# Gated linear attention ahead of a two-level expert layer: attention rebuilt chunk by chunk over all head pairs

## The chip, the cores and the metric

One core of one Trainium2 chip runs the program. The metric is the device time of one execution in microseconds (us); the time given for a kernel is the median of several runs, and the profile comes from one execution of its own.

## The reference

The first half is a gated linear attention over 4 batches, 8 heads, 768 positions and 48 values per head. The second is an expert layer over the 3072 tokens of width 384: a token picks one of 4 groups, then one of 4 experts in it, and goes through that expert's two matrices.

```python
for t in range(S):                       # attention, per batch and head
    state = alpha[t][:, None] * state + outer(k[t], v[t])
    y[t] = q[t] @ state
x = y as (B*S, H*D)
g_idx = argmax(x @ w_group); g_w = softmax value of it
e_idx = argmax(x @ w_expert[g_idx]); e_w = softmax value of it
out = g_w * e_w * (relu(x @ w1[g, e]) @ w2[g, e])
```

Everything is float32.

## The kernel before

**Attention.** The work is done in chunks of 128 positions, 6 to a batch, so that the recurrence becomes matrix products. Two heads share the partitions: one in 0 to 47, the other in 64 to 111 (`heads`, 112 partitions with the gap). The main loop (lines 339 to 362) runs over 16 combinations `j` of a batch and a pair of heads and does all six chunks of a pair before the next pair begins.

- `decayed(j)` (143) makes running products of the decays over 64-step segments with 12 scans (L150), their reciprocal over all 768 positions (L152), and from these the scaled queries and keys on VectorE and GpSimd: `qp` and `kp`, relative to a segment's start, `qs` and `ks`, relative to a chunk's, and `ka` for the second half of a chunk against the first (L155 to L175).
- `scores` (208) takes two chunks at a time: per head and chunk a 128x128 product (L214) and a 64x64 one over its upper right part (L216), both contracting over the 48 partitions of one head; VectorE applies the causal mask on the way out of the accumulator (L220).
- `states` (178) transposes the keys (L188), copies them to memory (L190), multiplies them with the values (L194), and runs the recurrence over the chunks in 48x48 pieces (L201, L203).
- `outputs` (226) adds the state's part (L232) and the scores' part (L237, 48 columns of values streamed against 128x128 masked scores) and copies the rows out (L241).
- `gates(b)` (244) comes once a batch, after its last pair: it transposes the rows (L250), takes the logits (L258), makes the choice of group and expert in some thirty small VectorE instructions (L269 to L323), counts each token's rank by two products (L310, L311), and scatters the rows, six tiles of 128, to the experts' slots in memory (L326).

A float32 product shows as two MATMUL rows with a weight load (LDWEIGHTS) each, a transpose as one.

**Experts.** Loop over 16 experts of 224 slots (425): `columns` transposes the fetched rows (L377), `hidden` does the first matrix (L390), `result` the second (L399), and a scatter writes the output (L404). Rows are fetched three experts ahead (L413).

**Order.** A scheduler fixes each engine's order ahead of time; within an engine instructions run in that order. The SyncE queue carries `load` (L141), the blanking of the slots (L348) and the weights (L120, L122); three experts' weights have buffers.

Of the kernel before, what the change touches and what calls it, by code (L numbers as in the profile page):

```python
# [20 lines left out]
SEG = 64  # L21
# [3 lines left out]
def gla_then_hierarchical_moe(  # L25
# [4 lines left out]
    wr_d: bass.AP,  # L30
    w1_d: bass.AP,
# [11 lines left out]

    nc = tc.nc
    B, H, D, _, S = qka_d.shape
    HP = H // 2
    D2 = 2 * D
    R = 64 + D
    NC = S // P
    NSEG = S // SEG  # L50
# [15 lines left out]
    wp = ctx.enter_context(tc.tile_pool(name="weights", bufs=3))  # L66
# [8 lines left out]
    slots_d = dp.tile([NE * N, XW], F32, name="slots_d")  # L75

# [13 lines left out]
    zeros = cp.tile([P, SEG], F32, name="zeros")  # L90
# [15 lines left out]
    wr = cp.tile([P, DC, NL], F32, name="wr")  # L106
# [20 lines left out]
    with ExitStack() as gla:  # L127
        NB = 2
        buf = gla.enter_context(tc.tile_pool(name="buf", bufs=1))
        prep = gla.enter_context(tc.tile_pool(name="prep", bufs=2))  # L130
        work = gla.enter_context(tc.tile_pool(name="work", bufs=3))
        qka = [buf.tile([P, 3, S], F32, name=f"qka{i}") for i in range(NB)]
        state = [buf.tile([P, NC - 1, D2], F32, name=f"state{i}") for i in range(NB)]
        for i in range(NB):
            nc.gpsimd.memset(qka[i], 1.0)
            nc.gpsimd.memset(state[i], 0.0)

        def load(j):
            b, hp = divmod(j, HP)
            for t in range(2):  # L140
                nc.sync.dma_start(out=qka[j % NB][heads[t]], in_=qka_d[b, 2 * hp + t])  # L141

        def decayed(j):
            t = qka[j % NB]
            q, k, a = (t[0:R, n, :] for n in range(3))
            cum = prep.tile([P, S], F32, name="cum")[0:R]
            inv = prep.tile([P, S], F32, name="inv", bufs=1)[0:R]
            for s in range(NSEG):
                sl = slice(s * SEG, (s + 1) * SEG)
                nc.vector.tensor_tensor_scan(out=cum[:, sl], data0=a[:, sl], data1=zeros[0:R],  # L150
                                             initial=1.0, op0=ALU.mult, op1=ALU.add)
            nc.vector.reciprocal(out=inv, in_=cum)  # L152
# [8 lines left out]
            def halves(z):  # L161
                z = z.rearrange("p (c h s) -> p c h s", h=2, s=SEG)
                return z[:, :, 0, :], z[:, :, 1, :]
# [175 lines left out]
        for j in range(PAIRS):  # L339
            b, hp = divmod(j, HP)  # L340
            if j + 1 < PAIRS:
                load(j + 1)
# [201 lines left out]
```

## Time and profile before

| | |
|---|---|
| median of 3 runs | 883.52 us (882.74 to 884.09) |
| profiled execution, its own time | 883.95 us |
| its span in the trace | 882.3 us |
| busy: PE, weight loads, VectorE (DVE), ScalarE (ACT), GpSimd (POOL) | 86%, 68%, 34%, 9%, 14% |
| moved by DMA | 90.29 MB |

Times inside the trace count from the start of the span. A busy PE is a modelled figure: a matmul row lasts from its issue to its modelled end and overlaps the next, so the pace of a row of matmuls is read from the distance of their starts.

### The profile page before, as it was taken

To read this page: it belongs to the slowest core of one execution; us is meant where nothing else is said; L and a number is where in the kernel's file an instruction comes from. 1 tells how busy PE (TensorE), PEld (TensorE's weight loads), DVE (VectorE), ACT (ScalarE), POOL (GpSimd) and SP (SyncE) were. 2 spreads that over 40 slices of the span, in tenths; PEclk is the share of its full clock that TensorE was granted. 3 is DMA by queue.
4 is the path that set the end of the run, shared out by engine and by line. 5 is a ranking of instruction groups with operands and counts; after the bars stand their busy time and mean duration, and the time that the engine had idled before them with its cause. 6 is when DMAs were issued, how large, how long until landed. Compare 5 with 4: busy or idle time off the path is not lost. (4 is left out here: it accounts for less than half of the span.)

```text
span 882.3 us, 8155 instructions
## 1 busy us (share of the span) xinstructions
PE 760.9 (86%) x3152; PEld 601.2 (68%) x3152; DVE 301.5 (34%) x805; ACT 80.0 (9%) x197; POOL 121.5 (14%) x126
## 2 busy tenths in 40 slices
PE   0099998799996999995999951999999999999995
PEld 0067777577775777784778741777777777777773
DVE  0466665625358434629253251011111111111100
ACT  0000111010010011010100000011111000001110
POOL 3111111032011121102300002010000001001000
PEclk9999999999999999999999999999999999999998
DMA  9844623230223030222000003255545554455100
GB/s 347 236 114 110 183 41 94 41 68 28 41 41 94 10 76 10 41 40 59 37 0 1 0 10 103 85 193 212 202 177 180 206 202 172 179 179 195 59 15 15
DMA packets 16646, 90.29 MB, mean 102 GB/s; under 512 B 2821, under 2 KB 6410, under 8 KB 10464
## 3 DMA queue, kind: packets, MB, share of 16 engines
q1 hardware_dynamic: 8464, 70.03, 26.1%
q10 hardware_dynamic: 4816, 10.29, 3.3%
q0 software_dynamic: 3328, 9.47, 3.0%
q8 instruction: 25, 0.41, 0.2%
q14 instruction: 13, 0.11, 0.0%
HBM read 74.77 MB, written 15.78 MB: 103 GB/s over the span
## 5 line engine op out<-in xcount | busy, mean ns | idle before, releaser
L214 PE MATMUL bank<-qp,kp 48*128 48x128 f32 x384 | 147.1, 498 | 43.8 <-DVE tot L175 43.8
L399 PE MATMUL bank<-w,hT 128*96 128x384 f32 (+1 forms) x512 | 168.2, 487 | 0.0
L390 PEld LDWEIGHTS bank<-xt_e,w 128*128 128x128 f32 x768 | 147.2, 193 | 5.7 <-issue 2.4
L390 PE MATMUL bank<-xt_e,w 128*128 128x224 f32 x768 | 150.4, 356 | 0.5 <-DVE xt_e L379 0.5
L214 PEld LDWEIGHTS bank<-qp,kp 48*128 48x128 f32 x384 | 92.5, 308 | 68.3 <-issue 47.3
L399 PEld LDWEIGHTS bank<-w,hT 128*96 128x96 f32 (+1 forms) x512 | 89.2, 177 | 70.0 <-issue 38.3
L237 PE MATMUL bank<-v,sm 128*128 128x48 f32 x384 | 98.0, 401 | 0.0
L237 PEld LDWEIGHTS bank<-v,sm 128*128 128x128 f32 x384 | 93.0, 330 | 4.8 <-issue 1.6
L220 DVE TENSOR_TENSOR sm<-bank,causal 128x256 f32<-128x256 f32 x96 | 39.8, 422 | 142.4 <-PE bank L216 141.1
L216 PE MATMUL bank<-qp,ka 48*64 48x64 f32 x384 | 87.5, 337 | 0.1
L216 PEld LDWEIGHTS bank<-qp,ka 48*64 48x64 f32 x384 | 52.6, 200 | 39.8 <-issue 38.1
L152 DVE RECIPROCAL inv<-cum 112x768 f32<-112x768 f32 x16 | 79.2, 4952 | 0.4
L402 DVE TENSOR_SCALAR yo<-bank,xg 128x384 f32<-128x384 f32 (+1 forms) x32 | 19.7, 615 | 154.1 <-PE bank L399 154.1
L404 POOL DMA_INDIRECT out_dram<-yo,dst x32 | 30.4, 950 | 300.2 <-DVE yo L402 300.2
L392 ACT ACTIVATE hT<-bank 128x448 f32<-128x448 f32 x64 | 34.8, 543 | 306.4 <-PE bank L390 306.4
L155 POOL TENSOR_TENSOR qp<-qka,cum 112x768 f32<-112x768 f32 x16 | 28.9, 1804 | 201.1 <-PE bank L216 62.5
L232 PE MATMUL bank<-state,qs 112*128 112x96 f32 x160 | 53.9, 456 | 0.0
L150 DVE TENSOR_TENSOR_SCAN cum<-qka,zeros 112x64 f32<-112x64 f32 x192 | 41.9, 274 | 32.3 <-DMA qka<-in_qka_dram 32.3
L194 PE MATMUL bank<-v,kn 128*112 128x96 f32 x160 | 39.9, 416 | 9.0 <-ACT kn L190 9.0
L194 PEld LDWEIGHTS bank<-v,kn 128*112 128x112 f32 x160 | 32.2, 298 | 16.4 <-ACT kn L190 14.5
L232 PEld LDWEIGHTS bank<-state,qs 112*128 112x128 f32 x160 | 41.3, 327 | 3.0 <-issue 1.1
L241 ACT COPY x<-bank 128x192 f32<-128x192 f32 x48 | 15.3, 320 | 275.6 <-PE bank L237 275.6
(103 smaller groups left out, 402.1 us busy)
## 6 DMA issues: line engine op xcount, KB each, us to landing
w<-in_w_dram SPq DMA_DIRECT2D x32, 1536.0 KB, 6.7
qka<-in_qka_dram SPq DMA_DIRECT2D x32, 432.0 KB, 6.6
slots_d<-blank SPq DMA_DIRECT2D x1, 5404.0 KB, 27.3
v<-in_v_dram ACTq DMA_DIRECT2D x4, 1152.0 KB, 5.2
xg<-slots_d ACTq DMA_DIRECT2D x16, 193.0 KB, 6.5
xg<-slots_d ACTq DMA_DIRECT2D x16, 144.8 KB, 6.3
out_dram<-yo,dst POOLq DMA_INDIRECT x32, 2.6
slots_d<-x,place POOLq DMA_INDIRECT x24, 2.9
```

Of the source, the lines that this page charges most:

```text
L150: nc.vector.tensor_tensor_scan(out=cum[:, sl], data0=a[:, sl], data1=zeros[0:R], initial=1.0, op0=ALU.mult, op1=ALU.add)
L152: nc.vector.reciprocal(out=inv, in_=cum)
L194: nc.tensor.matmul(z[0:R, c * D2:(c + 1) * D2], lhsT=kn[:, i, :], rhs=v[:, c, hp * D2:(hp + 1) * D2], start=True, stop=True)
L214: nc.tensor.matmul(z[:, o:o + P], lhsT=kp[r, c:c + P], rhs=qp[r, c:c + P], start=True, stop=True)
L216: nc.tensor.matmul(z[0:SEG, o + SEG:o + P], lhsT=ka[r, c // 2:c // 2 + SEG], rhs=qp[r, c + SEG:c + P], start=True, stop=True)
L220: nc.vector.tensor_tensor(out=s, in0=z[:, 0:2 * P].rearrange("p (c i) -> p c i", c=2), in1=causal[:, None, :].to_broadcast([P, 2, P]), op= ...
L232: nc.tensor.matmul(z[:, i * D2:(i + 1) * D2], lhsT=qs[:, c * P:(c + 1) * P], rhs=st[0:R, c - 1, :], start=True, stop=False, skip_group_che ...
L237: nc.tensor.matmul(z[:, i * D2 + t * D:i * D2 + (t + 1) * D], lhsT=sm[t][:, i, :], rhs=v[:, c, h * D:(h + 1) * D], start=(c == 0 and t == ...
L390: nc.tensor.matmul(z[:, k * n:(k + 1) * n], lhsT=w1[:, dc, f * P:(f + 1) * P], rhs=xt[:, dc, 0:n], start=(dc == 0), stop=(dc == DC - 1))
L392: nc.scalar.activation(out=hT[:, f0:f0 + 2, 0:n], in_=z[:, 0:2 * n].rearrange("p (f t) -> p f t", f=2), func=AF.Relu)
L399: nc.tensor.matmul(zy[0:n, 0:DM], lhsT=hT[:, f, c0:c0 + n], rhs=w2[:, f, :], start=(f == 0), stop=(f == FC - 1))
L404: nc.gpsimd.indirect_dma_start(out=out, out_offset=bass.IndirectOffsetOnAxis(ap=dst, axis=0), in_=yo[0:n], in_offset=None, bounds_check=N ...
```

## The change

The attention is rewritten; the expert part keeps its instructions.

- **Input layout.** The host packs a unit of three chunks (half a batch) of a head pair into 112 partitions: queries, keys, decays with a zero at each chunk's first position, and those first decays apart. The loop runs over 24 chunks `n`; each does all four head pairs.
- **Decays.** `decayed(u, p)` uses two scans of 384 positions: one backwards, relative to the chunk's end (`rev`), one forwards that begins at its reciprocal (`cq`). The reciprocal is taken of three values. Keys times `rev` and queries times `cq` are two GpSimd products; ScalarE copies the queries of each head into a tile `qb` that is zero in the other head's partitions.
- **Scores.** One product per head pair and chunk: 112 partitions, both heads side by side in 256 columns. The 64x64 products go; a mask covers 512 columns.
- **State and outputs.** One state tile for all pairs; the update is two additions and two multiplications. The outputs come out transposed (48 rows of a head by 128 positions), with the values as weights.
- **Rows and logits** come from one product per pair with a matrix that holds a selector and the routing weights (`to_rows`); the transposes and copies of `gates` go.
- **Routing** of the last batch is cut into groups of 3, 2 and 1 tiles, `choose` and `send` are apart, and the scatters write to views that are declared disjoint.
- **Weights** have two buffers in place of three; those of expert e+2 are asked for between `hidden(e)` and `result(e)`.

```diff
-    wp = ctx.enter_context(tc.tile_pool(name="weights", bufs=3))
+    wp = ctx.enter_context(tc.tile_pool(name="weights", bufs=2))
...
+    slots_by_tile = dram_disjoint_views(slots_d, NT)
...
+        def decayed(u, p):
...
+            nc.vector.tensor_tensor_scan(out=flat(rev)[:, ::-1], data0=az[:, US:0:-1],
+                                         data1=flat(ends)[:, ::-1], initial=0.0,
+                                         op0=ALU.mult, op1=ALU.add)
+            nc.vector.reciprocal(out=st[:, :, 0], in_=rev[:, :, 0])
+            nc.vector.tensor_tensor_scan(out=flat(cq), data0=az[:, 0:US], data1=flat(st),
+                                         initial=0.0, op0=ALU.mult, op1=ALU.add)
+            nc.vector.tensor_tensor(out=tot[:, :, p], in0=rev[:, :, 0], in1=a0, op=ALU.mult)
+            nc.gpsimd.tensor_tensor(out=flat(kp[:, p]), in0=k, in1=flat(rev), op=ALU.mult)
+            nc.gpsimd.tensor_tensor(out=flat(qp[:, p]), in0=q, in1=flat(cq), op=ALU.mult)
+            for i, r in enumerate(heads):
+                nc.scalar.copy(out=qd[r, p, :, i, :], in_=qp[r, p])
...
+        def scores(n):
...
+                    nc.tensor.matmul(z[:, (p - g) * 2 * P:(p - g + 1) * 2 * P],
+                                     lhsT=kp[:, p, c, :],
+                                     rhs=qd[:, p, c].rearrange("r h s -> r (h s)"),
+                                     start=True, stop=True)
+                nc.vector.tensor_tensor(out=sm[:, 2 * g:2 * g + 4, :],
+                                        in0=z.rearrange("p (h i) -> p h i", h=4),
+                                        in1=causal[:, None, :].to_broadcast([P, 4, P]),
+                                        op=ALU.mult)
...
+        def next_state(n, st):
...
+            for p in range(HP):
+                nc.tensor.transpose(zt[:, p * R:(p + 1) * R], kp[:, p, c, :], ident[0:R, 0:R])
+            nc.scalar.copy(out=kt, in_=zt[:, 0:HP * R])
...
+                nc.tensor.matmul(z[0:R, p * D2:(p + 1) * D2], lhsT=kt[:, p * R:(p + 1) * R],
+                                 rhs=v[:, bc, p * D2:(p + 1) * D2], start=True, stop=True)
...
+                nc.vector.tensor_tensor(out=new[r, :, cols], in0=st[r, :, cols],
+                                        in1=add[r, :, i, :], op=ALU.add)
+                nc.vector.tensor_tensor(
+                    out=new[r, :, cols], in0=new[r, :, cols],
+                    in1=tot[r, n % UC, :, None].to_broadcast([D, HP, D]), op=ALU.mult)
...
+        def outputs(n, sm, st):
...
+                nc.tensor.matmul(z[0:R, p * P:(p + 1) * P], lhsT=st[:, p, :], rhs=qp[:, p, c, :],
+                                 start=(p == 0), stop=False, skip_group_check=True)
...
+                    nc.tensor.matmul(z[r, p * P:(p + 1) * P],
+                                     lhsT=vs[b][:, bc, h * D:(h + 1) * D], rhs=sm[:, h, :],
+                                     start=False, stop=True, skip_group_check=True)
...
+        def to_rows(n, yt):
...
+                nc.tensor.matmul(z[:, p * W:(p + 1) * W], lhsT=yt[:, p, :], rhs=wr[:, p, :],
+                                 start=True, stop=True)
...
+        cuts = [0, NC // 2, NC - 1, NC]
+        for c0, c1 in zip(cuts, cuts[1:]):
+            groups[(B - 1) * NC + c1 - 1] = (B - 1, c0, c1)
...
         hT = hidden(w1, xt, CAP)
+        if e + 2 < NE:
+            load_weights(e + 2, e + 2)
...
-        if e + 3 < NE:
-            load_weights(e + 3, e + 3)
```

TensorE (PE) in the attention, before: two chunks' scores of one pair end here and the next pair's begin. Numbers tell tiles apart.

```order
L232 MATMUL bank_249<-state0_118,qs_152 128x96
L237 MATMUL bank_249<-v_126,sm0_232 128x48
L237 MATMUL bank_249<-v_126,sm1_239 128x48
L214 MATMUL bank_289<-qp_275,kp_276 128x128
L214 MATMUL bank_296<-qp_275,kp_276 128x128
L216 MATMUL bank_289<-qp_275,ka_281 64x64
L214 MATMUL bank_289<-qp_275,kp_276 128x128
L216 MATMUL bank_289<-qp_275,ka_281 64x64
L216 MATMUL bank_296<-qp_275,ka_281 64x64
L214 MATMUL bank_296<-qp_275,kp_276 128x128
L216 MATMUL bank_296<-qp_275,ka_281 64x64
```

The same engine after the change, one chunk from its keys' transposes on (L218 transposes, L224 keys by values, L265 rows and logits, L200 scores, L244 and L249 outputs):

```order
L218 MATMUL bank_619<-ident_73,kp_397 128x112 x4
L224 MATMUL bank_626<-v_298,kt_620 112x96 x4
L265 MATMUL bank_635<-wr_100,yt_563 128x116 x4
L200 MATMUL bank_718<-qb0_124,kp_397 128x256 x2
L200 MATMUL bank_722<-qb0_124,kp_397 128x256 x2
L244 MATMUL bank_726<-qp_396,state2_128 112x128 x4
L249 MATMUL bank_726<-sm_595,v_298 48x128 x8
```

Four kinds of product of 48 to 128 columns that alternate have become runs of four or eight of one kind; the longest stretch without a wait for ScalarE is rows, scores and outputs.

VectorE (DVE) in the attention, before, from the scans of one pair to those products that end the next pair's preparation (scans print as SCALAR_TENSOR_TENSOR here):

```order
L150 SCALAR_TENSOR_TENSOR cum_390<-qka0_116,zeros_86 112x64 x10
L296 COPY x_774<-token_f_90 128x6
L152 RECIPROCAL inv_391<-cum_390 112x768
L201 COPY state1_119<-bank_303 48x48 x2
L203 SCALAR_TENSOR_TENSOR state1_119<-state1_119,tot_287,bank_303 48x48 x8
L220 TENSOR_TENSOR sm0_338<-bank_333,causal_78 128x256
L220 TENSOR_TENSOR sm1_345<-bank_340,causal_78 128x256
L220 TENSOR_TENSOR sm0_359<-bank_354,causal_78 128x256
L220 TENSOR_TENSOR sm1_366<-bank_361,causal_78 128x256
L156 TENSOR_TENSOR kp_406<-qka0_116,inv_391 112x768
L173 TENSOR_TENSOR qs_409<-qp_405,cum_390 112x6x64
L170 TENSOR_TENSOR ks_410<-kp_406,cum_390 112x6x64
```

VectorE after the change, around one mask (L204) and one state update (L230):

```order
L181 SCALAR_TENSOR_TENSOR rev_399<-qka_289,ends_119 112x384
L184 RECIPROCAL starts0_122<-rev_399 112x3
L187 TENSOR_TENSOR tot_398<-rev_399,qka_289 112x3
L185 SCALAR_TENSOR_TENSOR cq_400<-qka_289,starts0_122 112x384
L204 TENSOR_TENSOR sm_349<-bank_354,causal_78 128x512
L181 SCALAR_TENSOR_TENSOR rev_409<-qka_291,ends_119 112x384
L184 RECIPROCAL starts1_123<-rev_409 112x3
L187 TENSOR_TENSOR tot_398<-rev_409,qka_291 112x3
L185 SCALAR_TENSOR_TENSOR cq_410<-qka_291,starts1_123 112x384
L181 SCALAR_TENSOR_TENSOR rev_466<-qka_293,ends_119 112x384
L230 TENSOR_TENSOR state2_128<-state1_127,bank_380 48x4x48 x2
```

The large reciprocal is gone; masks and state updates stand between the scans of the next unit.

SyncE's queue at the program's start, before:

```order
L120 DMA w1_386<-in_w1_dram 128x3072
L348 DMA slots_d_72<-blank_103 112x16x772
L141 DMA qka0_116<-in_qka_dram 48x2304 x2
L141 DMA qka1_117<-in_qka_dram 48x2304 x2
L122 DMA w2_387<-in_w2_dram 128x3072
```

And after the change:

```order
L157 DMA qka_136<-in_qka_dram 112x1156
L157 DMA qka_138<-in_qka_dram 112x1156
L157 DMA qka_140<-in_qka_dram 112x1156
L157 DMA qka_142<-in_qka_dram 112x1156
L157 DMA qka_189<-in_qka_dram 112x1156
L397 DMA slots_d_72<-blank_103 112x16x772
```

The first unit's four inputs and one of the second now stand ahead of the 5404 KB of blanking; a matrix of weights and the blanking stood ahead of the first input before.

## Rows read from the trace of the kernel before

**Rows 1.** Stretches: length, busy (count) of PE, PEld, DVE, ACT, POOL; PEclk, DMA, GB/s.
```profile
0.00:43.80 43.80, 0.04 (x1) 0.07 (x1) 9.61 (x20) 1.79 (x2) 8.99 (x24) 1.00 0.88 293
43.80:515.70 471.90, 434.15 (x1762) 351.31 (x1763) 242.14 (x634) 42.99 (x129) 76.27 (x65) 1.00 0.22 53
515.70:548.20 32.50, 3.13 (x17) 2.84 (x15) 11.78 (x58) 0.45 (x2) 5.84 (x6) 1.00 0.15 49
548.20:882.30 334.10, 323.53 (x1376) 247.03 (x1376) 37.99 (x95) 34.78 (x64) 30.40 (x32) 0.99 0.42 153
```

**Rows 2.** Groups of PE at 548 us, then at 561 us: count, busy us, mean ns, idle.
```profile
L377 PE MATMUL bank<-ident,xg 128*128 128x128 f32 x3 | 0.9, 430 | 25.4 <-DMA xg<-slots_d 25.4
...
L377 PE MATMUL bank<-ident,xg 128*128 128x128 f32 x3 | 0.5, 273 | 0.0
```

**Rows 3.** Two stretches of 4.6 us in expert 0's L390, same columns.
```profile
550.10:554.70 4.60, 4.60 (x12) 4.20 (x13) 0.23 (x2) 0.00 (x0) 0.00 (x0) 1.00 0.35 97
555.10:559.70 4.60, 4.60 (x26) 4.60 (x25) 0.00 (x0) 1.04 (x3) 0.00 (x0) 1.00 0.00 0
```

**Rows 4.** Timeline of PE in the attention: start us, length us, what.
```profile
131.16 0.79 PE L214 MATMUL bank<-qp,kp 48*128 48x128 f32 x2
131.88 0.47 PE L216 MATMUL bank<-qp,ka 48*64 48x64 f32 x2
132.28 0.79 PE L214 MATMUL bank<-qp,kp 48*128 48x128 f32 x2
...
144.88 1.93 PE L250 MATMUL bank<-ident,x 128*128 128x128 f32 x8
...
152.78 4.03 PE L258 MATMUL bank<-wr,xt 128*128 128x20 f32 x18 [2.84 <-DVE xt L254]
...
167.27 0.63 PE L188 MATMUL bank<-ident,ks 112*128 112x112 f32 x2
168.39 1.06 PE L194 MATMUL bank<-v,kn 128*112 128x96 f32 x4 [0.49 <-ACT kn L190]
```

**Rows 5.** Groups of VectorE by line and shape, whole span.
```profile
L220 DVE TENSOR_TENSOR sm<-bank,causal 128x256 f32<-128x256 f32 x96 | 39.8, 422 | 142.4 <-PE bank L216 141.1
L203 DVE SCALAR_TENSOR_TENSOR state<-state,tot,bank 48x48 f32<-48x48 f32 x128 | 33.6, 263 | 4.1
L150 DVE TENSOR_TENSOR_SCAN cum<-qka,zeros 112x64 f32<-112x64 f32 x192 | 41.9, 274 | 32.3 <-DMA qka<-in_qka_dram 32.3
L449 DVE TENSOR_TENSOR_SCAN ends<-more,zeros 128x16 f32<-128x16 f32 x1 | 0.2, 182 | 0.0
L152 DVE RECIPROCAL inv<-cum 112x768 f32<-112x768 f32 x16 | 79.2, 4952 | 0.4
```

**Rows 6.** Single lines: shortest, median and longest ns of one.
```profile
L170 DVE TENSOR_TENSOR ks<-kp,cum x16: 547/550/1197, 43.8 to 479.1; 112x384 f32<-112x384 f32 x16
...
L175 DVE TENSOR_TENSOR tot<-cum x16: 160/164/799, 43.5 to 480.2; 112x6 f32<-112x6 f32 x16
```

**Rows 7.** A group of GpSimd, whole span.
```profile
L169 POOL TENSOR_TENSOR ka<-kp,cum 112x384 f32<-112x384 f32 x16 | 15.4, 960 | 156.0 <-DVE kp L156 151.6 <-DVE tot L175 4.4
```

**Rows 8.** Timeline of the start, all engines but PE.
```profile
4.95 19.33 SPq L141 DMA_DIRECT2D qka<-in_qka_dram  x4
...
35.07 2.29 DVE L150 TENSOR_TENSOR_SCAN cum<-qka,zeros 112x64 f32<-112x64 f32 x12 [32.27 <-DMA qka<-in_qka_dram]
```

**Rows 9.** Timeline of the last batch's routing.
```profile
518.52 0.28 DVE L261 COPY lg<-bank 128x120 f32<-128x120 f32 x1 [1.75 <-PE bank L258]
...
542.53 0.97 POOL L326 DMA_INDIRECT slots_d<-x,place  x1 [2.14 <-DMA slots_d<-x,place]
545.23 3.70 ACTq L413 DMA_DIRECT2D xg<-slots_d  x8
...
548.19 1.36 PE L377 MATMUL bank<-ident,xg 128*128 128x128 f32 x6 [25.35 <-DMA xg<-slots_d]
```

**Rows 10.** DMA issues: queue, count, size, median us to landing.
```profile
w<-in_w_dram SPq DMA_DIRECT2D x32, 1536.0 KB, 6.7
```

More of the change, by code (lines that the diff above doesn't have):

```diff
@@ L30, in gla_then_hierarchical_moe @@
     wr_d: bass.AP,
+    d_head: int,
     w1_d: bass.AP,
@@ L127, in gla_then_hierarchical_moe @@
     with ExitStack() as gla:
-        NB = 2
         buf = gla.enter_context(tc.tile_pool(name="buf", bufs=1))
+        inp = gla.enter_context(tc.tile_pool(name="inp", bufs=5))
         prep = gla.enter_context(tc.tile_pool(name="prep", bufs=2))
[L131 to L136, printed above, removed]
@@ new lines, in gla_then_hierarchical_moe @@
+        ends = buf.tile([R, UC, P], F32, name="ends")
+        nc.gpsimd.memset(ends, 0.0)
+        nc.gpsimd.memset(ends[:, :, P - 1:P], 1.0)
+        starts = [buf.tile([R, UC, P], F32, name=f"starts{i}") for i in range(2)]
+        qb = [buf.tile([R, HP, UC, 2, P], F32, name=f"qb{i}") for i in range(2)]
+        state = [buf.tile([R, HP, R], F32, name=f"state{i}") for i in range(3)]
+        for t in starts + state:
+            nc.vector.memset(t, 0.0)
+        nc.vector.memset(qb[0], 0.0)
@@ new lines, in scores @@
+        def scores(n):
+            u, c = divmod(n, UC)
+            _, kp, qd, _ = ready[u]
+            sm = work.tile([P, H, P], F32, name="sm")
+            for g in range(0, HP, 2):
+                z = bank()
+                for p in (g, g + 1):
+                    nc.tensor.matmul(z[:, (p - g) * 2 * P:(p - g + 1) * 2 * P],
[6 more added lines that the diff above has]
+                                        op=ALU.mult)
+            return sm
@@ L338, in gla_then_hierarchical_moe @@
-        load_v(0)
[L339 to L342, printed above, removed]
-            if hp == 0:
-                xs[b] = xp.tile([P, NC, XW], F32, name="x")
-                if b + 1 < B:
-                    load_v(b + 1)
-            if j == 1:
+                    out=slots_by_tile[b * NC + c0 + c],
+                    out_offset=bass.IndirectOffsetOnAxis(ap=place[:, c:c + 1], axis=0),
+                    in_=x[:, c0 + c, :], in_offset=None, bounds_check=NE * N - 1,
@@ new lines, in gla_then_hierarchical_moe @@
+        for p in range(HP):
+            load(0, p)
+        load_v(0)
+        for p in range(HP):
+            decayed(0, p)
+        for p in range(HP):
+            load(1, p)
+        LAST = B * NC
+        sm, st, yt = scores(0), state[0], None
+        for n in range(LAST):
+            u, c = divmod(n, UC)
+            if c == 0 and u + 1 < NU:
+                for p in range(0, HP // 2):
+                    decayed(u + 1, p)
+            elif c == 1 and u + 1 < NU:
+                for p in range(HP // 2, HP):
+                    decayed(u + 1, p)
+                if u + 2 < NU:
+                    for p in range(HP):
+                        load(u + 2, p)
+            if n == 1:
```

331 lines of the change are left out of this document (157 added, 174 removed).

## Prediction

> **What bounds the kernel now.** I read the busy time by stretch first [rows 1]. The reader is to see four stretches with different limits: 43.8 us before the first matmul, 471.9 us of attention in which PE is busy for 434, 32.5 us of routing in which PE does nothing, and 334.1 us of experts in which PE is busy for 323.5. The change rebuilds the first three. In the attention VectorE is busy for 242 us and waits for PE at every mask: L220 idles 142.4 us ahead of its 96 instructions [rows 5]. So PE sets the attention's length.
>
> The next question is at which clock PE did that. The clock column says 1.00 all along [rows 3], but the rows contradict it: the same transpose L377 takes 430 ns at 548 us and 273 ns at 561 us [rows 2], and L390 issues 12 matmuls in 4.6 us before 555 us and at least twice as many in the 4.6 us after [rows 3]. So for the time ahead of 555 us the column can't be taken at its word: there the engine was at the lower of its two levels (1.2 of 2.4 GHz). In the attention eight L250 transposes of that same 128x128 shape take 1.93 us, some 0.22 each and a drain [rows 4], the pace of the lower level by the price below. The attention ran at half clock.
>
> The pace at that level: L390 streams 224 columns in 4.6/12 = 0.38 us, that is 1.7 ns a column [rows 3]; L258 streams only 20 columns but loads 128 columns of weights, and 18 of them take 4.03 us, 0.22 each, again 1.7 ns for a loaded column [rows 4]. So I price a matmul row at 1.7 ns times the larger of streamed and loaded columns, and at half of it at the higher level. Two L214 and two L216 take 1.12 us from one L214 to the next [rows 4]; by this price they would take 2 x 0.22 + 2 x 0.11 = 0.66. The other 0.46 us goes with two changes of the products' shape (128 and 64 columns out of 48 partitions), 0.23 each.
>
> **The change, part by part.**
>
> *PE in the attention.* Per chunk and by this price at half clock (two rows a product, one a transpose): scores 8 rows of 256 columns, 3.5 us; state 8 of 128, 1.7; values 16 of 128, 3.5; rows and logits 8 of 128, 1.7; and for 20 of the 24 chunks 4 transposes, 0.9, and 8 rows of keys by values with 112 loaded columns, 1.5. That is 24 x 10.4 + 20 x 2.4 = 298 us. The value products have 48 output columns and stand between full ones: two changes of shape a chunk, 24 x 0.46 = 11 us. The keys' product waits for ScalarE's copy of the transposes: L194 starts 1.12 us after the two L188 before it, of which 0.49 is idle with a 224-column copy [rows 4]; with 448 columns, and the copy of the outputs ahead of it on ScalarE, I take 0.9 us, 20 x 0.9 = 18. Together 327 us at half clock; at the higher level 149 + 6 + 18 = 173 us, 7.2 a chunk.
>
> *Which level.* The only rise in the trace comes 4.9 us after L390's start, in a row of matmuls that stream without a gap [rows 3]. Nothing in the 472 us of attention is like it: L214 and L216 lose 0.46 of 1.12 us to changes of shape [rows 4], and L258 streams 20 columns while 128 load. After the change rows, scores, state and values follow one another for about 10 us at half clock, nearly all of it streaming. So I take it that the clock rises in the first chunks and mostly stays. The Trainium skill ("TensorE: Matmul & The Clock Gate", Part 1) says so as well: the slow level is the default and sustained activity releases it. By that rule PE is worth 173 us, without it 327.
>
> *VectorE in the attention* is then next. A scan goes from 182 ns for 16 steps to 274 for 64 [rows 5], 1.9 ns a step, so 384 steps take 0.9 us; a bound below is one step a ns, 0.5. With two scans, a reciprocal of three values and one small product (0.16 each, L175 [rows 6]) a pair costs 2.1 us. Beside them GpSimd does two products of 384 at 0.96 us [rows 7], more than it did there before, and rows show what that costs: L170 and L175 take up to 0.65 us longer than their shortest [rows 6]. For each of the two I take half of it: 0.65 a pair, bounds 0 and 1.3. The Trainium skill ("GPSIMD Engine Reference", section Specifications) puts it down to an SBUF interface that VectorE's two-input instructions share; the rows agree. 32 pairs x 2.75 = 88 us, 3.7 a chunk.
> Masks: 512 columns take between one and two L220 (0.42, 0.84 [rows 5]); I take 0.72, two a chunk, 1.4. The state: two additions and two multiplications on 192 columns against L203's 0.26 for 48 [rows 5]; between 0.26 and 1.05, I take 0.4 and 0.3, 1.4 together. The logits' sum 0.3. Routing: from 518.5 to 526.7 us [rows 9] some 7.5 us of small instructions a group, five groups inside the loop, 37 us, 1.5 a chunk. Sum 8.3 us a chunk, 199 us. The reciprocals that go (16 x 4.95 = 79 us [rows 5]) were covered by PE.
>
> So VectorE with 8.3 and PE with 7.2 us pace a chunk together, in a fixed order in which masks and state updates stand between scans. L220 waits 142.4/96 = 1.5 us on average now [rows 5]; some such wait will stay each chunk. I take 1.2: 9.5 us a chunk, 228 us.
>
> *The start.* The first scan waits for its input until 35.07 us, issued at 4.95 behind a matrix of weights and the blanking [rows 8]. After the change four inputs of 518 KB go first; with the fifth and two 1152 KB loads of v about 5.1 MB move in front of the blanking, at 293 GB/s [rows 1] 17 us, the first pairs sooner. PE starts at about 17 us (13 to 24) instead of 43.8. But the second unit's other three inputs stand behind the blanking: 12.1 MB in all, 41 us, and then their preparation, while three chunks from 17 us end at 45. I take 4 us of waiting there, 0 to 10.
>
> *Routing of the last batch.* From 518.52 to 548.19 us [rows 9], of which 526.7 to 543.5 are six scatters, each about 3.2 us after the last. One scatter is left at the end: 8 us of choice for one tile, 1, then 2.7 until the fetch and 3 for it [rows 9], 14 us in place of 32.5.
>
> *Experts.* The same instructions, 334.1 us. Weights of 1536 KB land in 6.7 us [rows 10]; w1 of expert e+2 is asked for when `hidden(e)` has ended and needed some 30 us later (an expert takes 334/16, about 21 us). I cost the third buffer's loss at nothing; PE's work on expert e+1 covers it, and without that cover it would be 7 us an expert.
>
> **Sum** against the profiled execution: 17 + (228 + 4) + 14 + 334 = 597 us of span, plus the 1.65 us that its time of 883.95 lies above its span: **599 us**. The median of the runs, 883.52, lies 0.4 below that execution, which changes nothing.
>
> **Rivals.**
>
> *The clock stays low in the attention.* For it: 472 us with PE never idle did not raise it [rows 1, 4], and the new products use 112 of the partitions and 48 of the outputs. Against it: the row of L390 that did raise it was no denser than the new stretch. PE then paces: 17 + 327 + 14 + 334 + 1.65 = 694 us, with VectorE's 199 hidden. A rule bears on its size. If the value products of two heads, which go to different columns of the array, can run side by side, half of their 24 x 3.5 = 84 us goes: 652. No row shows two products side by side. The Trainium skill ("TensorEngine Tiling (Array Packing)", section Tiling Modes) says that different tiles work in parallel, and that a change of mode drains the engine, which the 0.23 us agree with. In the forecast, where VectorE paces, this would change nothing.
>
> *Tighter overlap.* If GpSimd costs VectorE nothing and no wait stays, a chunk takes PE's 7.2 us: 17 + 173 + 14 + 334 + 2 = 540 us. Against it: rows 6.
>
> *Slower than before.* The backward scan, with negative steps over its operands, is shown by no row. VectorE sits at the head of every unit, so if such a scan were priced like the reciprocal, 4952/768 = 6.4 ns a step [rows 5], it would take 2.5 us, 32 x 1.6 = 51 us more: 650. It decides from about 25 ns a step on: 32 x 9.6 us less the 0.9 counted is 278 us more, 877 us and beyond. Nothing in the trace has such a price.
>
> *The second weight buffer too late:* 14 experts at up to 6.7 us, 94 us more, 693. Against it 30 us of slack.
>
> **How the numbers follow.** The forecast with its bounds (8.3 to 11 us a chunk: 199 or 264 in place of 228) holds 570 to 640 and has 0.60. Tighter overlap has 0.08, the clock that stays low 0.26 (645 to 700; 0.10 of it with the value products side by side), the late weights 0.04, the dear scan 0.02, half of it beyond the old time. The range 555 to 700 leaves out most of the tight case and the dear scan. This measurement can tell a change of 0.2% from none, 1.8 us: faster 0.98, same 0.01, slower 0.01.
>
> **What would show it.** Right: first matmul at 13 to 24 us; rows of the 256-column scores at about 0.21 us from start to start, and a clock record that starts before 100 us; VectorE busy most of the attention, some 8 us a chunk; PE's waits in it put down to VectorE; experts again 334 us. Wrong: scores 0.43 us apart to the end (the first rival); scans of 384 far from 0.9 us; PE waiting for weights between experts; idle time on PE in the attention that belongs to DMA beyond the second unit.

## The result, and the profile after

The changed kernel takes **592.89 us** (median of 4 runs, 591.61 to 593.77) against 883.13 (881.51 to 884.09): a ratio of 0.671, interval 0.670 to 0.673. Its profiled execution took 591.61 us with a span of 589.9. Times below are medians of several executions; one of the experiment with early inputs, 596.32 us, fell in a slower state and is left out.

The same four stretches as before the change (answering [rows 1]; length, busy time and count of PE, PEld, DVE, ACT, POOL, then PEclk, DMA share, GB/s):

```profile
0.00:15.75 15.75, 0.00 (x0) 0.03 (x1) 11.63 (x18) 2.42 (x4) 9.75 (x25) 1.00 0.89 273
15.75:241.90 226.15, 167.75 (x1210) 141.36 (x1210) 166.03 (x442) 66.95 (x139) 95.13 (x81) 0.89 0.44 147
241.90:256.50 14.60, 1.58 (x9) 1.22 (x8) 10.81 (x56) 0.89 (x3) 2.91 (x3) 0.50 0.38 117
256.50:589.90 333.40, 322.76 (x1370) 246.37 (x1370) 37.08 (x93) 34.77 (x64) 30.41 (x32) 0.98 0.45 161
```

The attention shrank from 471.9 to 226.15 us, and no engine is busy throughout it: PE 74%, VectorE 73%. The experts kept their length: their first transpose now stands at 254.75, so 335.2 us against 334.1. Of the 292 us by which the span shrank, 28 come off the start, 246 off the attention and 20 off the last routing; the experts gave back 1.

The timeline of PE shows both levels of the clock (answering [rows 4]): scores at half clock in the first chunks, then one chunk at full clock.

```profile
25.64 4.61 PE L200 MATMUL bank<-qb,kp 112*128 112x256 f32 x10 [0.49 <-ACT qb L191]
30.04 1.34 PE L244 MATMUL bank<-qp,state 112*112 112x128 f32 x8
...
218.23 1.90 PE L200 MATMUL bank<-qb,kp 112*128 112x256 f32 x8
219.97 1.04 PE L244 MATMUL bank<-qp,state 112*112 112x128 f32 x8
220.93 1.08 PE L249 MATMUL bank<-sm,v 128*48 128x128 f32 x16
221.95 0.60 PE L218 MATMUL bank<-ident,kp 112*128 112x112 f32 x4
223.22 1.02 PE L224 MATMUL bank<-v,kt 128*112 128x96 f32 x8 [0.68 <-ACT kt L219]
224.09 1.07 PE L265 MATMUL bank<-wr,yt 112*128 112x116 f32 x8
225.00 1.90 PE L200 MATMUL bank<-qb,kp 112*128 112x256 f32 x8
```

From 25.64 to 30.04 ten 256-column rows go by at 0.44 us each; at 218 us eight take 1.74, 0.22 each. A chunk at full clock with nothing late takes 6.77 us, 0.68 of it the wait for the copy of the keys. Twenty-four of those are 162 us. What makes 226 of them? The waits of PE (15 to 242 us; what for: total, times, longest):

```profile
PE bank L200 <- ACT qb L191: 29.3, 5, 15.8
PE bank L224 <- ACT kt L219: 28.3, 20, 4.9
PE bank L244 <- DVE state L232: 11.6, 7, 3.3
PE bank L337 <- DVE picked L319: 3.5, 1, 3.5
```

The longest of the first line, 15.8, is the start itself. Inside the attention PE idles 58.4 us (226.15 less 167.75): 13.5 for prepared queries, 28.3 for the keys' copy, 11.6 for the state. The rest is clock:

```profile
30.70:194.50 163.80, 122.32 (x879) 103.42 (x879) 125.18 (x290) 48.56 (x99) 72.89 (x63) 0.85 0.49 158
194.50:238.90 44.40, 34.85 (x304) 30.47 (x304) 29.42 (x126) 14.43 (x33) 12.44 (x11) 1.00 0.08 28
```

The clock rises at 30.7 us, just behind the row of scores above, but until 194.5 it alternates (mean 0.85). It first falls at 44.3, inside a wait of 6.25 us; from 194.5 on, where the last unit's preparation is all but done and PE waits 7 us in 44, it stays high. At full clock the products need at most 24 x (6.77 - 0.68) = 146 us, PE was busy for 167.75: at least 21 us are the half clock. At half clock throughout, the same products would keep PE busy for up to twice that, 292 us, against 434 before the change. So by this estimate the new products took some 142 us off PE and the higher clock another 124; no run separates the two.

VectorE by groups in the attention (count | busy us, mean ns | idle before them; answering [rows 5, 6]):

```profile
L185 DVE TENSOR_TENSOR_SCAN cq<-qka,starts 112x384 f32<-112x384 f32 x30 | 37.1, 1238 | 0.5
L204 DVE TENSOR_TENSOR sm<-bank,causal 128x512 f32<-128x512 f32 x48 | 32.0, 680 | 7.3 <-PE bank L200 7.0
L181 DVE TENSOR_TENSOR_SCAN rev<-qka,ends 112x384 f32<-112x384 f32 x30 | 31.8, 1066 | 8.8 <-POOL kp L188 6.4 <-DMA qka<-in_qka_dram 2.3
L187 DVE TENSOR_TENSOR tot<-rev,qka 112x3 f32<-112x3 f32 x30 | 14.2, 487 | 0.2
L230 DVE TENSOR_TENSOR state<-state,bank 48x192 f32<-48x192 f32 x40 | 13.9, 348 | 23.8 <-PE bank L224 23.1
```

Where the second unit's preparation stands shows in the timelines of VectorE, GpSimd and PE:

```profile
40.59 0.73 DVE L230 TENSOR_TENSOR state<-state,bank 48x192 f32<-48x192 f32 x2 [3.16 <-PE bank L224]
42.40 0.96 DVE L181 TENSOR_TENSOR_SCAN rev<-qka,ends 112x384 f32<-112x384 f32 x1
43.39 0.18 DVE L184 RECIPROCAL starts<-rev 112x3 f32<-112x3 f32 x1
43.49 0.96 DVE L187 TENSOR_TENSOR tot<-rev,qka 112x3 f32<-112x3 f32 x1
...
43.44 0.99 POOL L188 TENSOR_TENSOR kp<-qka,rev 112x384 f32<-112x384 f32 x1 [16.38 <-DVE x L323]
...
48.16 1.19 PE L200 MATMUL bank<-qb,kp 112*128 112x256 f32 x2 [6.25 <-ACT qb L191]
```

VectorE's order puts the scan of the second pair (42.40) behind two chunks' state updates, for which it waits on PE; then PE waits on it. The new unit's scores go pair by pair as the pairs become ready: PE's rows for them start at 41.30, 48.16, 50.74 and 55.75 us. And L187, whose output is three values wide, takes 0.96 us: it begins 0.05 us after GpSimd's product and ends with it (44.45 against 44.43).

The tail, answering [rows 9]: the last rows, the last scatter, the first transpose of the experts.

```profile
239.88 2.03 PE L265 MATMUL bank<-wr,yt 112*128 112x116 f32 x8
...
248.67 0.97 POOL L353 DMA_INDIRECT slots_d<-x,place  x1 [2.99 <-DVE n_more L531]
...
254.75 1.35 PE L430 MATMUL bank<-ident,xg 128*128 128x128 f32 x6 [8.78 <-DMA xg<-slots_d]
```

### The profile page after: what moved, and what is told of

Its sections match the earlier page's. It is cut to its first block, busy times and chain, and to the rows that moved or that the text cites. A ratio compares the mean times of both kernels' runs of the same rounds, so it can differ in the third digit from the quotient of the medians.

```text
span 589.9 us, 6890 instructions
## 1 busy us (share of the span) xinstructions
PE 492.1 (83%) x2588; PEld 389.0 (66%) x2588; DVE 225.6 (38%) x607; ACT 105.0 (18%) x209; POOL 138.2 (23%) x141
## 5 line engine op out<-in xcount | busy, mean ns | idle before, releaser
L200 PE MATMUL bank<-qb,kp 112*128 112x256 f32 x192 | 58.4, 453 | 30.7 <-ACT qb L191 29.3
L200 PEld LDWEIGHTS bank<-qb,kp 112*128 112x128 f32 x192 | 41.9, 233 | 39.6 <-issue 18.2
L189 POOL TENSOR_TENSOR qp<-qka,cq 112x384 f32<-112x384 f32 x32 | 42.3, 1331 | 50.0 <-PE bank L244 33.0
L188 POOL TENSOR_TENSOR kp<-qka,rev 112x384 f32<-112x384 f32 x32 | 37.3, 1178 | 45.1 <-DVE rev L181 17.3
L224 PE MATMUL bank<-v,kt 128*112 128x96 f32 x160 | 22.9, 292 | 28.3 <-ACT kt L219 28.3
L191 ACT COPY qb<-qp 48x384 f32<-48x384 f32 x64 | 32.6, 510 | 64.6 <-POOL qp L189 63.9
L224 PEld LDWEIGHTS bank<-v,kt 128*112 128x112 f32 x160 | 19.3, 196 | 32.6 <-ACT kt L219 32.6
L185 DVE TENSOR_TENSOR_SCAN cq<-qka,starts 112x384 f32<-112x384 f32 x32 | 39.7, 1244 | 0.5
L181 DVE TENSOR_TENSOR_SCAN rev<-qka,ends 112x384 f32<-112x384 f32 x32 | 33.7, 1059 | 10.8 <-POOL kp L188 6.4
L244 PE MATMUL bank<-qp,state 112*112 112x128 f32 x192 | 27.6, 291 | 11.6 <-DVE state L232 11.6
L244 PEld LDWEIGHTS bank<-qp,state 112*112 112x112 f32 x192 | 25.8, 191 | 15.7 <-issue 10.8
L204 DVE TENSOR_TENSOR sm<-bank,causal 128x512 f32<-128x512 f32 x48 | 32.0, 680 | 7.3 <-PE bank L200 7.0
L265 PE MATMUL bank<-wr,yt 112*128 112x116 f32 x192 | 31.4, 316 | 0.0
```

The source lines that it names most:

```text
L181: nc.vector.tensor_tensor_scan(out=flat(rev)[:, ::-1], data0=az[:, US:0:-1], data1=flat(ends)[:, ::-1], initial=0.0, op0=ALU.mult, op1=ALU ...
L185: nc.vector.tensor_tensor_scan(out=flat(cq), data0=az[:, 0:US], data1=flat(st), initial=0.0, op0=ALU.mult, op1=ALU.add)
L188: nc.gpsimd.tensor_tensor(out=flat(kp[:, p]), in0=k, in1=flat(rev), op=ALU.mult)
L189: nc.gpsimd.tensor_tensor(out=flat(qp[:, p]), in0=q, in1=flat(cq), op=ALU.mult)
L191: nc.scalar.copy(out=qd[r, p, :, i, :], in_=qp[r, p])
L200: nc.tensor.matmul(z[:, (p - g) * 2 * P:(p - g + 1) * 2 * P], lhsT=kp[:, p, c, :], rhs=qd[:, p, c].rearrange("r h s -> r (h s)"), start=Tr ...
```

## The experiments

Three theories of the attention: **A**, VectorE paces it, slowed by GpSimd; **B**, the chain scan, GpSimd product, ScalarE copy, scores paces it; **C**, PE paces it. All ratios are to the kernel before, run beside; differences are to the changed kernel's 592.9 unless another is named.

**Products on VectorE.**

```diff
-            nc.gpsimd.tensor_tensor(out=flat(kp[:, p]), in0=k, in1=flat(rev), op=ALU.mult)
-            nc.gpsimd.tensor_tensor(out=flat(qp[:, p]), in0=q, in1=flat(cq), op=ALU.mult)
+            nc.vector.tensor_tensor(out=flat(kp[:, p]), in0=k, in1=flat(rev), op=ALU.mult)
+            nc.vector.tensor_tensor(out=flat(qp[:, p]), in0=q, in1=flat(cq), op=ALU.mult)
```

> The changed kernel with the two GpSimd products of a pair (keys by rev, queries by cq) moved to VectorE; nothing else. Theory A (VectorE paces the attention, slowed by GpSimd's products beside it): VectorE gets 64 products of about 0.55 us, 35 us more, and loses the slowing, so the scans, now 1.06 and 1.24 us on average, fall to 0.95 and the small product from 0.49 to 0.14: 25 us less; the time moves by no more than 15 us either way, 585 to 608. Theory B (the chain from scan over GpSimd and ScalarE to the scores sets the pace, VectorE's load doesn't): a link of 1.0 to 1.7 us becomes 0.55 and GpSimd's queue goes out of the chain: 560 to 582. Theory C (PE paces): within 3 us of the changed kernel.

569.12 us (566.82 to 573.24; ratio 0.643, 0.641 to 0.645): 24 us faster. VectorE by groups, 15 to 250 us:

```profile
L185 DVE TENSOR_TENSOR_SCAN cq<-qka,starts 112x384 f32<-112x384 f32 x30 | 28.4, 948 | 0.1
L181 DVE TENSOR_TENSOR_SCAN rev<-qka,ends 112x384 f32<-112x384 f32 x30 | 27.6, 940 | 2.9 <-DMA qka<-in_qka_dram 2.9
L188 DVE TENSOR_TENSOR kp<-qka,rev 112x384 f32<-112x384 f32 x30 | 16.2, 547 | 1.5 <-PE bank L218 1.0 <-remote 0.5
...
L187 DVE TENSOR_TENSOR tot<-rev,qka 112x3 f32<-112x3 f32 x30 | 4.1, 143 | 0.2
```

Sixty products (30 each) cost VectorE 32 us, and its scans and L187 give back 23 of them (37.1 + 31.8 + 14.2 to 28.4 + 27.6 + 4.1). The product takes 0.55 us here and took 1.2 to 1.3 on GpSimd, so the chain from scan to scores is some 0.6 to 0.8 us shorter at each product. VectorE has more to do (169.4 us busy in place of 166.0) and the kernel is faster, so A alone falls.

**Scores twice**, the second set into a spare bank that nothing reads.

```diff
+            spare = bank()
+            for p in range(HP):
+                o = p % 2 * 2 * P
+                nc.tensor.matmul(spare[:, o:o + 2 * P], lhsT=kp[:, p, c, :], ...
```

> The changed kernel with the four score products of every chunk done a second time into a spare bank that nobody reads. PE gets 24 x 8 rows of 0.21 us, 41 us at the higher clock level. Theory C (PE paces): 625 to 645. Theories A and B (PE waits 58 us of the attention's 226 for others): most of it disappears in these waits, 593 to 610; and if the low stretches of the clock record (17 stretches change level during the attention) come from PE's waits, they get fewer, since PE waits less.

618.4 us (615.37 to 619.21; 0.699, 0.697 to 0.701): 25.5 us slower. PE's timeline:

```profile
210.01 1.90 PE L200 MATMUL bank<-qb,kp 112*128 112x256 f32 x8
211.75 1.89 PE L211 MATMUL bank<-qb,kp 112*128 112x256 f32 x8
213.47 1.04 PE L250 MATMUL bank<-qp,state 112*112 112x128 f32 x8
```

The copy takes 1.72 us a chunk (213.47 less 211.75), 41 us in all, of which 60% shows. Neither C (all) nor A and B (next to none) hold; PE and the preparation take turns at being late. On the clock the expectation was not met: PE idles 47 us in place of 58, yet the clock falls ten times before the attention ends, as in the changed kernel; it is low for 44 us in place of 51.

**Scores per head** out of 48 partitions, without the padded query tile and ScalarE's copies into it.

```diff
-                nc.scalar.copy(out=qd[r, p, :, i, :], in_=qp[r, p])
...
+                    nc.tensor.matmul(zs[i][:, p * P:(p + 1) * P], lhsT=kp[r, p, c, :],
+                                     rhs=qp[r, p, c, :], start=True, stop=True)
```

> One part undone: the scores are computed per head over its own 48 partitions (eight products of 128 columns a chunk, the two heads alternating, each head into a bank of its own), so the zero-padded query tile and ScalarE's 64 copies of 0.51 us go. Theory B: the wait of PE for those copies (29.3 us) goes for the most part: 562 to 578. Theory A: VectorE's load is the same, 583 to 594. If products of the two heads on different partitions run side by side as those of the values now do (16 rows in 1.0 us), the 16 score rows take about 1.1 us a chunk instead of 1.9; if they run one after the other with changes of shape, about 2 us.

590.32 us (585.75 to 591.47; 0.668, 0.667 to 0.669): 2.6 us faster. PE's timeline, then its waits from 15 us on, behind the start:

```profile
203.17 1.16 PE L195 MATMUL bank<-qp,kp 48*128 48x128 f32 x16
204.26 1.13 PE L238 MATMUL bank<-qp,state 112*112 112x128 f32 x8
```

```profile
PE bank L238 <- DVE state L226: 24.5, 11, 4.6
PE bank L218 <- ACT kt L213: 17.7, 18, 4.3
PE bank L195 <- POOL qp L186: 15.3, 7, 5.9
```

The scores are shorter by 0.65 us a chunk at full clock (1.09 in place of 1.74) and a link of the chain is gone, 15.6 us in all, yet almost nothing comes of it. PE's busy time fell by only 8 us (167.75 to 159.7), with a mean clock of 0.86 in place of 0.89, and the wait for the state grew from 11.6 to 24.5 us. Relief at one place went into the next wait and into the clock.

**The same with the second unit's inputs early**: eight input buffers, which the room of the padded tile allows, so that its four inputs go ahead of the blanking.

```diff
-        inp = gla.enter_context(tc.tile_pool(name="inp", bufs=5))
+        inp = gla.enter_context(tc.tile_pool(name="inp", bufs=8))
```

> The split scores of the kernel before this one, and eight buffers in place of five for the inputs of the head pairs, so that the first two units' inputs all stand ahead of the blanking in SyncE's queue. In the changed kernel the third and fourth chunk take 15.5 and 13.1 us from state product to state product against some 8 later. If that is the wait for inputs behind the blanking: 10 to 14 us less than with the split scores alone. If it is the preparation itself (VectorE, GpSimd): within 4 us of it.

589.36 us (587.23 to 593.58; 0.666, 0.664 to 0.667): no gain over the step before. The second unit's first chunk comes later, not earlier: its state product (L238) starts at 64.93 us in place of 56.34. Data behind the blanking is not what stalls the first unit.

**Both: products on VectorE and scores per head.**

```diff
-                nc.scalar.copy(out=qd[r, p, :, i, :], in_=qp[r, p])
...
-            nc.gpsimd.tensor_tensor(out=flat(kp[:, p]), in0=k, in1=flat(rev), op=ALU.mult)
+            nc.vector.tensor_tensor(out=flat(kp[:, p]), in0=k, in1=flat(rev), op=ALU.mult)
...
```

> The two products of the decays move from GpSimd to VectorE, and the scores are taken per head out of 48 partitions, with no padded query tile and no ScalarE copies (the two edits tried alone before, 569.1 and 590.3 us). Theory A (the gains add, each edit shortens its own link): 569.1 - 2.6 = 566.5 us, 563 to 570. Theory B (with the products on VectorE the ScalarE copy is the next link, its wait is still 27.0 us in that run, and it now goes with nothing in its place): 545 to 560 us, and TensorE's wait for the preparation under 10 us. Theory C (TensorE's own pace is next: the split scores are 16 rows a chunk of 128 columns with changes of shape in place of 8 of 256): 570 to 585 us.

567.45 us (566.12 to 573.56; 0.644, 0.640 to 0.648). That lies in A's range, but so does the 569.12 (0.643) of the products alone, and the two can't be told apart: that the gains add isn't shown. B's time is not there, though its wait is (9.9 us for the preparation, behind the start); the wait for the state grew from 7.2 to 12.5 us. C, 570 to 585, is missed by the median and holds the slowest run. B rested on a misreading of mine: of the 27.0 us that PE waited for the copy with the products on VectorE, 14.2 were the start.

**Keys' product alone on VectorE.**

```diff
-            nc.gpsimd.tensor_tensor(out=flat(kp[:, p]), in0=k, in1=flat(rev), op=ALU.mult)
+            nc.vector.tensor_tensor(out=flat(kp[:, p]), in0=k, in1=flat(rev), op=ALU.mult)
```

> Only the keys' product moves to VectorE; the queries' stays on GpSimd. With both moved the time fell from 592.9 to 569.1 us. Theory A (what GpSimd costs is that it slows VectorE's instructions; half of it stays): 578 to 584 us, VectorE's small product L187 at 0.25 to 0.40 us on average (0.487 with both on GpSimd, 0.143 with none). Theory B (what it costs is its link in the chain scan, product, copy, scores; the queries' product is the one on that link and stays): 586 to 594 us. Theory C (the queries' waits for the tile's earlier readers hold up the keys' behind them on GpSimd's queue, and that goes): 566 to 575 us.

581.29 us (579.25 to 582.11; 0.657, 0.656 to 0.659): half of the 24 us, with L187 at 0.287 us, both as A has it. VectorE by groups:

```profile
L181 DVE TENSOR_TENSOR_SCAN rev<-qka,ends 112x384 f32<-112x384 f32 x30 | 31.2, 1052 | 3.1 <-DMA qka<-in_qka_dram 3.1
L185 DVE TENSOR_TENSOR_SCAN cq<-qka,starts 112x384 f32<-112x384 f32 x30 | 28.4, 948 | 0.6
L187 DVE TENSOR_TENSOR tot<-rev,qka 112x3 f32<-112x3 f32 x30 | 8.2, 287 | 0.2
```

The scan during which the keys' product used to run is back at 0.95 us; the backward scan, beside which the queries' product still runs, is not. So GpSimd costs VectorE only what starts while a product runs, and then up to that product's whole time. The Trainium skill ("SBUF — State Buffer", section "SBUF: two separate sides") states it so: one of the two engines holds the shared ports for a whole instruction and the other is blocked. The row of L187 above, 0.96 us for three values and ending with the product, agrees. The run does not show that this slowing is all of the 24 us: the keys' product is also a link of the chain and a place in GpSimd's queue, and both went with it.

**Preparation late**: with the products on VectorE, each chunk's share of it comes behind that chunk's other work in the program's order.

```diff
-                for p in range(0, HP // 2):
-                    decayed(u + 1, p)
...
+            if c < 2 and u + 1 < NU:
+                for p in range(c * HP // 2, (c + 1) * HP // 2):
+                    decayed(u + 1, p)
```

> Products of the decays on VectorE (569.1 us by itself) and, in the program's order, a chunk's share of the next unit's preparation behind that chunk's scores, outputs and state in place of ahead of them; the same instructions. Theory A (a large part of what is left is masks and state updates that stand behind scans in VectorE's fixed order): TensorE's waits for the copy of the keys and for the state, 26 us together in the run without the reorder, fall by half, 552 to 562 us. Theory B (what stands first only changes which engine waits; the preparation then comes later by as much): 564 to 576 us, with the wait for the preparation above the 27 us it had.

563.66 us (561.41 to 567.44; 0.638, 0.637 to 0.639), 5.5 below 569.1 and between the two theories. PE's wait for the keys' copy fell from 19.3 to 16.6 us and that for the state rose from 7.2 to 8.7, so the halving that A named is not there; its wait for the preparation rose from 27.0 to 28.3, as B has it, but the time did not. Inconclusive.

**Early preparation**: scores per head, products on VectorE, the early inputs, and all of the second unit prepared in the first chunk.

```diff
...
-                for p in range(0, HP // 2):
+                for p in range(0, HP if n == 0 else HP // 2):
...
```

> Products on VectorE and split scores (567.5 us by themselves), eight input buffers, the second unit's inputs ahead of the blanking, and all four pairs of the second unit prepared in the first chunk of the first unit in place of two in each of the first two chunks. VectorE then has something to do in the stretch from 31 to 42 us in which it idles 7.8 us ahead of state updates. Theory A (the stall of the first unit is this order alone): 557 to 563 us, and no step between chunks above 11 us in the first unit but one longer first step. Theory B (the later units, which follow without such idle time, set the pace and take it back): 564 to 571 us. Theory C (the inputs now compete with the values and the second unit's come late): over 571 us.

**554.45 us** (553.22 to 559.84; 0.627, 0.626 to 0.628), below all three ranges. It looked like A, until the next run took the edit out again:

**Inputs alone** (against the step before).

```diff
-                for p in range(0, HP if n == 0 else HP // 2):
+                for p in range(0, HP // 2):
...
```

> Products on VectorE, split scores, eight input buffers and the second unit's inputs ahead of the blanking, but two pairs of the second unit prepared in each of the first two chunks, as in the changed kernel: the step before (554.5 us) without its early preparation. Theory A (the early preparation makes the gain; in the run on GpSimd products the inputs alone brought nothing): 564 to 569 us, as without the inputs (567.5). Theory B (the inputs make the gain: with them there the schedule puts six scans of the second unit ahead of the second chunk's masks of itself): 553 to 559 us.

555.29 us (553.25 to 556.72; 0.628, 0.627 to 0.629): the same time. The gain of 12 us over 567.45 belongs to the input buffers, B. But its place is not the one I had in mind. PE's timeline at the fifth chunk's and the last chunk's state product, without the early inputs:

```profile
61.77 1.10 PE L238 MATMUL bank<-qp,state 112*112 112x128 f32 x8 [1.12 <-DVE state L226]
...
208.15 1.94 PE L238 MATMUL bank<-qp,state 112*112 112x128 f32 x8
```

and with them:

```profile
63.51 1.13 PE L238 MATMUL bank<-qp,state 112*112 112x128 f32 x8
...
199.34 1.10 PE L238 MATMUL bank<-qp,state 112*112 112x128 f32 x8 [0.78 <-DVE state L226]
```

The start is 1.7 us later, not earlier; the 19 chunks after it take 135.8 us in place of 146.4. The second unit's first chunk is again later (L238 at 55.13 us in place of 52.50). With more input buffers the schedule gives VectorE another order in all units, and PE's wait for the preparation behind the start falls from 9.9 to 4.4 us. Which part of that order does it was not tried, nor why the same buffers brought nothing on top of GpSimd's products.

**Values apart**: the four value products of one head position, then the four of the other, in place of alternating.

```diff
-            for p in range(HP):
-                for i, r in enumerate(heads):
+            for i, r in enumerate(heads):
+                for p in range(HP):
```

> The eight value products of a chunk in another order: the four of the heads in columns 0 to 47 of the array first, then the four in columns 64 to 111; in the changed kernel the two kinds alternate. Theory S (neighbouring products to different columns run side by side; the 16 rows take 1.0 us at full clock in the changed kernel, 0.063 each): rows of one kind 0.10 to 0.11 us apart, 16 of them about 1.7 us, 0.7 us a chunk, 17 us of TensorE in all, of which some 60% shows by the doubled scores' run: 603 us, 598 to 610. Theory N (a row with 48 output columns is simply cheap): 16 rows still about 1.0 us, time 590 to 595 us.

600.61 us (599.09 to 601.05; 0.679, 0.677 to 0.680), 7.7 us slower. PE's timeline:

```profile
225.90 1.55 PE L249 MATMUL bank<-sm,v 128*48 128x128 f32 x16
227.38 0.60 PE L218 MATMUL bank<-ident,kp 112*128 112x112 f32 x4
```

Sixteen rows now take 1.48 us and took 1.02 (220.93 to 221.95), 0.093 against 0.064 each: neighbours that write different columns of the array run side by side, theory S, though a row apart costs less than the 0.107 I gave it. The scores per head did the same from the side of the partitions: 16 rows of 128 columns in 1.09 us. The Trainium skill ("TensorEngine Tiling (Array Packing)", section Tiling Modes) states that different tiles work in parallel; the trace agrees. Of 24 x 0.46 = 11 us added, 70% shows.

**One group at the end**: the last batch's routing uncut.

```diff
-        cuts = [0, NC // 2, NC - 1, NC]
+        cuts = [0, NC]
```

> The last batch's routing as one group of six tiles at the end, as it was before the change; the scatters still go to views declared disjoint. Theory A (the cut saves the scatters behind the last choice, now 1.27 us apart): five more scatters, 6.4 us, and about 1 us for a wider choice, less what VectorE saves in the last three chunks: 598 us, 595 to 602, first transpose of the experts 6 to 8 us later after the last chunk's rows. Theory B (the tail is the choice alone, its two earlier groups cost VectorE as much inside the loop as they save at the end): 589 to 594 us.

601.64 us (598.44 to 602.15; 0.679, 0.677 to 0.681), 8.7 us slower, theory A. PE's timeline at the end of the attention:

```profile
242.95 2.04 PE L265 MATMUL bank<-wr,yt 112*128 112x116 f32 x16
...
266.20 1.35 PE L430 MATMUL bank<-ident,xg 128*128 128x128 f32 x6 [16.90 <-DMA xg<-slots_d]
```

From the end of the rows to the experts: 21.2 us in place of 12.8, 8.4 more where A had 6 to 8.

**Plain views**: the scatters write to the whole array again.

```diff
-                    out=slots_by_tile[b * NC + c0 + c],
+                    out=slots_d,
```

> The scatters of the rows write to the whole array of slots again in place of views declared disjoint. One scatter then waits for the one before it, some 3.2 us in place of 1.27. Theory A (the waits hold up GpSimd's queue, and with it the products of the decays that stand behind them: 18 scatters inside the loop at up to 1.9 us each, about a third to all of 35 us): 602 to 628 us. Theory B (the products stand elsewhere in the order, and with one scatter in the last group the tail hardly changes): 590 to 597 us.

610.28 us (609.71 to 610.42; 0.690, 0.689 to 0.691), 17.4 us slower, in A's range but only in part by its mechanism. GpSimd's last scatters and PE's first transpose of the experts:

```profile
264.84 0.97 POOL L353 DMA_INDIRECT slots_d<-x,place  x1 [2.58 <-DMA slots_d<-x,place]
268.23 0.97 POOL L353 DMA_INDIRECT slots_d<-x,place  x1 [2.42 <-DMA slots_d<-x,place]
...
273.80 1.35 PE L430 MATMUL bank<-ident,xg 128*128 128x128 f32 x6 [20.56 <-DMA xg<-slots_d]
```

Some 7 us are lost before the attention ends (its last rows end at 249.0 in place of 241.9), where A had 12 to 35; PE waits 36.6 us there for the copy of the keys in place of 28.3, and whether GpSimd's queue is behind that was not followed. The other 12 are in the tail, which neither theory had, where scatters 3.4 us apart from the last two batches still stand in a row. A tail with a single group of one tile doesn't help if older scatters queue ahead of it: the cut and the views are needed together.

## Why the prediction was right, and where it was not

The time came out 6 us below the forecast of 599. Its terms against the trace: start 15.75 (17), attention 226.15 (232), tail 12.85 (14), experts 335.15 (334.1). Inside the attention VectorE's work came out 33 us below the forecast and the waits 27 above it: two steps failed and cancelled each other, and that the sum came so close is luck.

- **PE's prices** held: 0.44 and 0.22 us for 256 columns at the two levels, 0.12 for the state's rows (0.107). The value products came out at 1.0 us a chunk where one after the other would be 1.7; the prediction had the side-by-side case in a rival only. A chunk is 6.77 us at full clock, forecast 7.2.
- **VectorE's sum** was to be 199 us, and VectorE was busy for 166. The durations of its 442 rows add to 187 us: decays 89 (88), masks 33 (34), state 29 (34), logits 5 (7), routing 31 (37). The step that failed first is the adding itself. A short row starts before the one ahead of it has ended (above, L184 starts at 43.39 and takes 0.18, and L187 starts at 43.49), so 187 us of durations fill 166 us of time. The rest is mostly *routing, 1.5 a chunk, 37 us in all*. The stretch of the kernel before that it was read from is nearly all busy, but eight of its 44 rows (L369 to L478, 2.8 us) prepare the experts and stand behind the loop after the change as well:

```profile
518.52:526.70 8.18, 0.34 (x2) 0.13 (x2) 7.36 (x44) 0.45 (x2) 0.04 (x1) 1.00 0.00 1
```

- **The waits** were to be 24 x 1.2 + 4 = 33 us; VectorE was idle for 60 of 226. The failed step is *I take 4 us of waiting there, 0 to 10*: the second unit's first chunk began 28.6 us after the second chunk (36.27 and 64.86 for L244), where two steps of 6.8 would be 13.6, so 15 us. I made the inputs responsible. With early inputs that chunk came later than without them (64.93 against 56.34 us, 55.13 against 52.50), so the inputs don't hold it. What is left is the unit's preparation itself, which shares VectorE's fixed order with masks and state updates (the scan at 42.40 above). The preparation was spread evenly in the sum, but all four pairs must be through it before a unit's first chunk can end.
- **Who paces** was put as VectorE and PE together in a fixed order. That no engine paces alone holds: added PE work shows at 60 to 70%, relief of PE (15.6 us by scores per head) at a sixth, and moving work *to* VectorE gained 24 us. That *PE's waits are put down to VectorE* does not: 28.3 us go to ScalarE's copy of the keys, and 13.5 to the chain through GpSimd and ScalarE.
- **The clock** was to rise in the first chunks and mostly stay. It rose right behind the second chunk's scores and then fell nine times before 194.5 us; at least 21 us of PE's time come of it. So a part of the first rival is in the result. What makes it fall is not shown: with the scores doubled and with the products on VectorE, PE idles 47 and 46 us of the attention, and the clock falls ten and five times, for 44 and 38 us in all.
- **GpSimd's price**, half of 1.3 us a pair, was near: (1.238 - 0.948) + (1.066 - 0.940) + (0.487 - 0.143) = 0.76 against 0.65.
- **Scans** take 0.94 us alone (0.9), also the backward one, so that rival is gone. **Weights** with two buffers show no cost beyond the 1 us by which the experts grew, and no wait of PE for weights stands in the trace. The **tail** stood for the reason given, but needs both of its edits.

## What to carry to other kernels

Where no engine is busy throughout, price the waits as carefully as the work: list what must be complete before each unit's first chunk can end. The durations of short rows do not add up to an engine's load where they overlap, 187 us against 166 here; look at their starts, and see that a stretch holds only the work that you price. A helper engine that holds up the busy one may be no relief: here the same products were cheaper on the busy engine itself, 569 us against 593. When a second edit rides along with one that gains, take it out again before believing it.

## What the runs showed of the hardware that was not expected

A VectorE instruction of three values takes as long as the GpSimd product beside which it starts: 0.96 us in place of 0.14. Float32 products that use different halves of the array's columns, or of its partitions, take 0.064 and 0.068 us a row of 128 columns when they alternate, against 0.12 for the state's rows that span both; with the same half twice running a row took 0.093. And the clock column reads 1.00 ahead of the first change on record: it has 1.00 for the stretch from 15.75 to 30.70 us, in which the rows at 25.64 us go by at 0.44 us each, twice what they take later. Runs of the kernel before that agree within 0.2% carry mean clocks from 0.767 to 0.997.
